# Windowed attention with a routed feed-forward: dilated values loaded on all partitions, their weights written at four offsets

## The chip, the cores and the metric

The kernel runs on one core of a Trainium2 chip. The metric is the device time of one execution in microseconds (us), as the median of several runs. Engines: PE is TensorE (matmuls; PEld is its weight load), DVE is VectorE, ACT is ScalarE, POOL is GpSimd, SP only issues DMAs.

## The reference

Eight batches of eight heads, 576 tokens, 64 dimensions per head, all float32. Heads 0 to 3 attend to the last 32 tokens ("plain"); heads 4 to 7 attend to 32 tokens that are 4 apart ("dilated"). Then, in each batch, the 128 tokens with the highest gate score go through a feed-forward layer, and the result is added to their rows.

```python
rel = pos[:, None] - pos[None, :]
mask_plain = (rel >= 0) & (rel < 32)
mask_dil = (rel >= 0) & (rel < 32 * 4) & (rel % 4 == 0)
scores = np.where(mask, scale * q @ k.T, -1e9)
attn = softmax(scores)
x = (attn @ v).transpose(0, 2, 1, 3).reshape(8, 576, 512)
...
scores = np.einsum('bsd,d->bs', x, w_gate)
for b in range(8):
    top_idx = np.argpartition(-scores[b], 128)[:128]
    ye = np.maximum(x[b, top_idx] @ w1, 0.0) @ w2      # 512 -> 1024 -> 512
    out[b, top_idx] = x[b, top_idx] + sigmoid(scores[b, top_idx])[:, None] * ye
```

## The kernel before

The tokens of the dilated heads are sorted by their residue modulo 4, so that dilated attention too is a band of 32. Every batch has five units u of 128 queries by four heads: u = 0 and 1 are dilated (two residues each), u = 2 and 3 plain, u = 4 holds the last rows of both kinds. A unit works on groups of 32 queries, each of which sees at most 64 keys.

A unit goes through these steps. `scores` (S, lines 300 to 309) writes the mask into PSUM by four matmuls and adds 16 products of q and k (in the trace a float32 matmul is two instructions, so 32). `maximum` and `subtract` (MX, SU) on DVE take the row maximum off. `turn` (TR, line 327) transposes with four matmuls. `exps` (EX, line 334) lets ACT write the exponentials into one of two buffers `pt`, whose other halves were set to zero at the start: keys 0 to 63 of one half of the groups lie on partitions 0 to 63, those of the other half on partitions 64 to 127. `attend` (V, line 347) multiplies with the values on all 128 partitions, two groups at a time; a column of ones beside the values gives the divisor. `divisors` (DN), then the division on DVE (XM) or ACT (XA), `store` (ST) to HBM on SP's queue, and the gate score (GM on POOL and GA on ACT, or GD on DVE alone).

The values of a dilated unit lie in `vd` (tile tag v1), which holds the 128 last keys of each residue twice, in the second copy moved by 32 partitions, so that a group's 64 keys always meet the partitions that its weights lie on. It is filled by four DMAs of 64 partitions (line 287). `vp` (tag v0, line 283) holds the plain values with overlap, `vl` (line 280) the first keys of each residue for u = 4. Loads of q, values and half of k are issued on SP's queue, the other half of k on ACT's. Every tile of q, k (one per kind), vd and vp has one buffer. SP and ACT issue in program order, and eight completion semaphores ("slots") serve all their DMAs in turn: a DMA waits for the one that used its slot last.

When the scores of a batch b are complete, the routing ranks them (RX, RO, SC, SP, SB, RK, RC, RA, MK or MV, PK, IX), `gather` (GT, line 486) fetches the 128 rows from HBM into `xe` by an indirect DMA on POOL's queue, XT transposes them on PE, and XH and XL split them into a high and a low part. Batches are put together as GROUP lines say: F, HH, HL (pairs) or N, RL, HT, HI, HO (single ones) compute the first layer, Y the second, three matmuls for each piece. `result` (YO, line 590) frees `xe`, and `scatter` (SY) writes the rows back. LW, WH or WV, and WL load and split the weights. W n runs n idle matmuls (line 603), which compute nothing.

The order of all this is the table `ORDER`, written out by hand into the file as the output of a planner: the program text follows the table entry by entry, and every engine and queue runs its share in that order.

Of the kernel before, what the change touches and what calls it, by code (L numbers as in the profile page):

```python
# [51 lines left out]
DN 0 4, VL 1 0, GD 0 1, TR 1 0, W 5, GM 0 0, MX 1 1, EX 1 0, SU 1 1, GM 0 2, S 1 3, GA 0 0, XM 0 4, LW 1, GM 0 3,
TR 1 1, GA 0 2, MX 1 3, S 1 4, W 2, RX 0, EX 1 1, SU 1 3, LW 4, GM 0 4, MX 1 4, TR 1 3, K 2 1 1, SU 1 4, S 1 2,
GA 0 3, ST 0 4, TR 1 4, GA 0 4, MX 1 2, V 1 0, SU 1 2, K 2 0 1, WV 1, TR 1 2, EX 1 3, VL 1 1, WV 4, RO 0, WL 1,
DN 1 0, XM 1 0, SC 0, V 1 1, GD 1 0, ST 0 3, WL 4, VL 1 2, SP 0, EX 1 2, DN 1 1, XM 1 1, K 2 1 0, SB 0, GD 1 1, LW 3,
RK 0 0, V 1 2, W 8, LW 2, RK 0 1, EX 1 4, Q 2 1, RK 0 2, RK 0 3, RK 0 4, K 2 0 0, DN 1 2, RC 0, W 2, XM 1 2, WH 3,
ST 1 0, RA 0, V 1 4, GM 1 2, VL 2 0, MV 0, WV 2, PK 0, WL 3, GA 1 2, DN 1 4, S 2 0, IX 0, RX 1, SG 0, XM 1 4, S 2 1,
MX 2 0, ST 1 1, GT 0, SU 2 0, V 1 3, MX 2 1, GM 1 4, TR 2 0, W 3, LW 5, DN 1 3, SU 2 1, EX 2 0, WL 2, XM 1 3, TR 2 1,
Q 2 0, EX 2 1, SH 0, V 2 0, GD 1 3, ST 1 4, GA 1 4, DN 2 0, XT 0, XM 2 0, XH 0, RO 1, GM 2 0, WH 5, V 2 1, XL 0,
LW 7, SC 1, GA 2 0, N 0 0 0, ST 1 3, WL 5, DN 2 1, VL 2 1, S 2 4, SP 1, XA 2 1, MX 2 4, S 2 2, SU 2 4, WV 7, LW 6,  # L60
TR 2 4, MX 2 2, WL 7, S 2 3, SB 1, VL 2 2, SU 2 2, K 3 1 1, N 0 0 1, RK 1 0, EX 2 4, Q 3 1, TR 2 2, RK 1 1, N 0 1 0,
# [675 lines left out]
```

## Time and profile before

| | us |
|---|---|
| time, median of 3 runs (298.64 to 309.14) | 302.31 |
| time of the profiled execution | 297.06 |
| its span, first to last instruction | 295.1 |
| PE busy | 261.2 |
| DVE busy | 166.2 |
| ACT busy | 120.3 |
| POOL busy | 92.5 |

The mean granted PE clock is 0.955 of full speed. The DMA engines moved 57.53 MB. Engines overlap, and a busy share is a mean over stages; waits are read from the stage in which they stand. Matmuls are pipelined, so a busy PE isn't PE at its peak. The releaser named beside an idle time is the one that came last by the profile.

### The profile page before, as it was taken

The numbers are of one execution on the slowest core, as the hardware profiler recorded it, in microseconds if no ns is written. First come the engines' busy times: TensorE is split into PE (matmuls) and PEld (weight loads), VectorE is DVE, ScalarE is ACT, GpSimd is POOL, SyncE is SP. The second block draws the span as 40 slices with busy tenths as digits, with TensorE's granted clock in tenths as the row PEclk, the third lists the DMA queues.
The fourth block names the chain that finished last, engine by engine and source line by source line (L and its number), as shares of the span: only waits on it lengthen the run. The fifth ranks groups of instructions, "written<-read, shape, count | busy, mean of one in ns | idle before, by whom it ended". The sixth has DMA issues, their size and how long they took to land.

```text
span 295.1 us, 8991 instructions
## 1 busy us (share of the span) xinstructions
PE 261.2 (88%) x3738; PEld 216.6 (73%) x3738; DVE 166.2 (56%) x442; ACT 120.3 (41%) x337; POOL 92.5 (31%) x106
## 2 busy tenths in 40 slices
PE   5778785597998999959999979999999999999992
PEld 1465554565876888748879868888878998998881
...
DMA  6998995999999999887995997994422300200000
GB/s 187 228 291 225 328 283 101 278 322 314 334 292 261 269 312 254 242 242 212 239 359 143 278 279 188 318 233 124 174 72 92 109 0 2 71 36 2 36 36 36
DMA packets 24791, 57.53 MB, mean 195 GB/s; under 512 B 3632, under 2 KB 14512, under 8 KB 23728
## 3 DMA queue, kind: packets, MB, share of 16 engines
q1 hardware_dynamic: 21696, 47.96, 56.5%
...
## 4 chain that ended last, share of the span: by engine, by line
PE 34%; DMA 33%; issue 18%; DVE 6%; POOL 3%; ACT 2%; SPq 1%; POOLq 0%; ACTq 0%; DVEq 0%
DMA k<-in_kt_dram 16%; PE a L347 8%; DMA vp<-in_va_dram 8%; PE s L309 6%; PE py L585 6%; DMA out_dram<-x 5%; PE t L327 3%; PE ph L542 3%; DMA xe<-out_dram,ix 3%; DMA q<-in_qt_dram 3%; PE pi L466 2%; PE s L303 2%; ACT x L366 2%; DVE rm L438 1%; POOL out_dram L595 1%
## 5 line engine op out<-in xcount | busy, mean ns | idle before, releaser
L334 ACT ACTIVATE pt<-t 64x512 f32<-64x512 f32 x80 | 47.4, 592 | 69.7 <-PE t L327 51.4
L390 POOL TENSOR_TENSOR gm<-x,wg 128x512 f32<-128x512 f32 x24 | 32.1, 1341 | 78.4 <-ACT x L366 28.5
L309 PE MATMUL s<-k,q 128*32 128x128 f32 (+2 forms) x1216 | 43.5, 276 | 7.3 <-DMA k<-in_kt_dram 5.4
L309 PEld LDWEIGHTS s<-k,q 128*32 128x32 f32 (+1 forms) x1216 | 36.4, 111 | 12.3 <-DMA k<-in_kt_dram 5.2
L314 DVE TENSOR_REDUCE mx<-s 128x8 f32<-128x512 f32 x40 | 27.5, 688 | 22.2 <-PE s L309 22.1
L347 PE MATMUL a<-vp,pt 128*64 128x65 f32 x640 | 29.8, 232 | 9.8 <-DMA vp<-in_va_dram 4.4
L347 PEld LDWEIGHTS a<-vp,pt 128*64 128x64 f32 x640 | 26.4, 144 | 15.9 <-issue 11.5
L366 ACT ACTIVATE x<-a,rin 128x64 f32<-128x64 f32 x104 | 22.8, 333 | 16.8 <-PE a L347 12.1
L542 PE MATMUL ph<-xh,w1h 128*128 128x256 f32 x96 | 28.6, 298 | 0.0
L542 PE MATMUL ph<-xh,w1l 128*128 128x256 f32 x96 | 27.5, 286 | 0.7 <-issue 0.7
L319 DVE TENSOR_TENSOR dt<-s,mx 128x512 f32<-128x512 f32 x40 | 27.1, 682 | 0.9
L542 PE MATMUL ph<-xl,w1h 128*128 128x256 f32 x96 | 27.4, 285 | 0.0
L585 PE MATMUL py<-w2h,hh 128*128 128x512 f32 x64 | 26.9, 420 | 0.0
L327 PE MATMUL t<-id,dt 128*128 128x128 f32 x160 | 25.3, 286 | 0.4 <-DVE rk L450 0.4
L585 PE MATMUL py<-w2l,hh 128*128 128x512 f32 x64 | 25.3, 395 | 0.0
L585 PE MATMUL py<-w2h,hl 128*128 128x512 f32 x64 | 25.3, 395 | 0.0
L347 PE MATMUL a<-vd,pt 128*64 128x65 f32 x512 | 20.2, 231 | 5.3 <-DVE ts L420 3.2
L400 ACT ACTIVATE junk<-gm 128x256 bf16<-128x256 f32 x48 | 20.1, 418 | 11.1 <-POOL gm L390 8.1
L347 PEld LDWEIGHTS a<-vd,pt 128*64 128x64 f32 x512 | 17.7, 143 | 8.6 <-issue 7.1
L460 POOL TENSOR_SCALAR oh<-slots_sb,rk 128x128 f32<-128x128 f32 x20 | 12.1, 618 | 32.5 <-DVE rk L450 32.5
L438 DVE SCALAR_TENSOR_TENSOR rm<-sb,ts,thr 128x576 bf16<-128x576 f32 (+3 forms) x32 | 20.5, 697 | 2.6 <-ACT sb L431 2.6
L327 PEld LDWEIGHTS t<-id,dt 128*128 128x128 f32 x160 | 18.3, 147 | 4.8 <-issue 1.6
...
## 6 DMA issues: line engine op xcount, KB each, us to landing
...
vd<-in_va_dram SPq DMA_DIRECT2D x32, 260.0 KB, 8.3
...
```

Source lines behind the costliest of these rows:

```text
L309: nc.tensor.matmul(st[G * a:G * a + m, e, g, :, lo:hi], qs[b, kind][:, g, q0:q0 + m], ks[kind][:, g::2, k0 + lo:k0 + hi], start=False, sto ...
L314: nc.vector.tensor_reduce(out=mx, in_=X["s", b, u].rearrange("p e g h k -> p (e g h) k"), axis=AX.X, op=ALU.max)
L319: nc.vector.tensor_tensor(out=dt.rearrange("p i (e k) -> p e i k", e=2), in0=st.rearrange("p e g h k -> p e (g h) k"), in1=mx.rearrange("p ...
L327: nc.tensor.transpose(tt[:, i * P:(i + 1) * P], dt[:, i, :], id32)
L334: nc.scalar.activation(pt[r, :, e], tt[r], AF.Exp, scale=SCALE)
L347: nc.tensor.matmul(av[r, a // 2, f], pt[:, i % 2, i // 2, a], values(b, u, a)[:, f], start=True, stop=True)
L366: nc.scalar.activation(xv[:, e, i], av[:, e, i, 0:D], AF.Copy, scale=rin[:, e, i:i + 1])
L390: nc.gpsimd.tensor_tensor(out=gm, in0=X["x", b, u], in1=gate_w(u), op=ALU.mult)
L400: nc.scalar.activation(junk, X["gm", b, u][:, c], AF.Copy, scale=UP, accum_out=acc)
L438: nc.vector.scalar_tensor_tensor(out=out, in0=X["sb", b][:, t * P:S], scalar=ts[:, b, t, 1:2], in1=thr[:, 0:n], op0=ALU.subtract, op1=ALU. ...
L542: nc.tensor.matmul(out, WS1[w][:, i, f * P:(f + 1) * P], X["x" + x, e][:, i, :], start=i == 0 and n == 0, stop=i == 3 and n == 2)
L585: nc.tensor.matmul(X["py", b], X["h" + x, e][:, i, j * P:(j + 1) * P], WS2[w][:, i, :], start=i == 0 and k == 0, stop=i == 7 and k == 2)
```

## The change

The dilated values are loaded once: one DMA fills 128 partitions with 128 keys of four residues, without a second copy. Since a group's 64 keys now lie at partitions 0, 32 or 64 onwards, the weights have to be written there, and `exps` does this for a dilated unit with five activations: two write 64 partitions, three write 32 of them, each 4 heads x 2 residues x 32 queries. The groups of a dilated unit are numbered anew for this, and the first group of each residue, which sees only 32 keys, is masked and computed on these alone. `pt` gets two buffers for dilated units and two for the others; those for dilated units are set to zero as a whole. `vl` gets its buffer from a list that `attend` of unit 4 gives back to. `xe` has three buffers instead of four. The mask and identity are loaded on POOL's queue instead of ACT's.

The table is another one. Its entries of attention and feed-forward are the same ones; the W entries hold 49 idle matmuls instead of 33, two more divisions stand on ACT, three more gate scores on DVE alone, and seven weight parts instead of three are cast on ACT. Of the table only the lines around the gather of batch 6 are shown.

```diff
--- before.py
+++ after.py
@@ -33,8 +33,9 @@
 EPS = 1e-9
 UP = 2.0 ** 24
 TINY = -2.0 ** -126
-BUFS = dict(q1=1, q0=1, v0=1, v1=1, s=2, a=1, m=4, dt=2, x=4, gm=2, xe=4, xh=1, hh=1, raw=2, y=2, oh=1, sb=1, xl=1, hl=1, mx=3, den=3, rin=3, rx=2, g=8, ix=8, junka=1, junkv=1)
+BUFS = dict(q1=1, q0=1, v0=1, v1=1, s=2, a=1, m=4, dt=2, x=4, gm=2, xe=3, xh=1, hh=1, raw=2, y=2, oh=1, sb=1, xl=1, hl=1, mx=3, den=3, rin=3, rx=2, g=8, ix=8, junka=1, junkv=1)
 WARM = 9
+NPT = (2, 2)
 
 
 
@@ -44,64 +45,64 @@
 GROUP 2 3 4
 GROUP 3 5 6
 GROUP 4 7
...
-SH 6, Y 1 6, XL 4, Y 1 7, F 2 0 0, YO 1, F 2 2 0, GT 6, V 7 3, GM 7 2, ST 7 2, F 2 0 1, DN 7 3, XA 7 3, SY 1,
...
+Y 4 4, ST 7 1, SH 6, Y 4 5, GA 7 1, Y 4 6, Y 4 7, RX 7, RO 7, YO 4, Y 3 0, SC 7, GT 6, SP 7, Y 3 1, SB 7, SY 4,
...
 """
 
@@ -140,7 +141,7 @@
     thr = cp.tile([P, S], F32, name="thr")
     ks = [cp.tile([P, 4, S], F32, name=f"k{i}") for i in range(2)]
     vls = [cp.tile([P, 2, VW], F32, name=f"vl{i}") for i in range(2)]
-    pts = [cp.tile([P, 16, 2, G], F32, name=f"pt{i}") for i in range(2)]
+    pts = [cp.tile([P, 16, 2, G], F32, name=f"pt{i}") for i in range(sum(NPT))]
     w1h = cp.tile([P, 4, FF], F32R, name="w1h")
     w1l = cp.tile([P, 4, FF], F32R, name="w1l")
     w2h = cp.tile([P, 8, DM], F32R, name="w2h")
@@ -154,14 +155,16 @@
 
     def constants(i):
         if i == 0:
-            nc.scalar.dma_start(out=mraw, in_=masks)
-            nc.scalar.dma_start(out=id32, in_=ident)
+            nc.gpsimd.dma_start(out=mraw, in_=masks)
+            nc.gpsimd.dma_start(out=id32, in_=ident)
             nc.vector.memset(warm, 0.0)
             nc.vector.memset(mk, NEG)
             for k in (1, 0):
                 nc.vector.memset(ks[k][0:HB, 2:4], 0.0)
                 nc.gpsimd.memset(ks[k][HB:P, 0:2], 0.0)
-            for t in pts:
+            for t in pts[:NPT[0]]:
+                nc.gpsimd.memset(t, 0.0)
+            for t in pts[NPT[0]:]:
                 for e in range(2):
                     nc.gpsimd.memset(t[HB * e:HB * (e + 1), :, 1 - e], 0.0)
 
@@ -170,7 +173,6 @@
                 nc.gpsimd.memset(v[HB + G:P], 0.0)
         elif i == 1:
 
-
             nc.vector.memset(id16, 0.0)
             nc.vector.tensor_copy(id16[0:G], id32[0:G, 0:G])
 
@@ -178,8 +180,8 @@
                 nc.vector.tensor_copy(o[:, :, lo:lo + src.shape[1]], src.unsqueeze(1).to_broadcast([P, o.shape[1], src.shape[1]]))
 
             d, p = mraw[:, 0:GK], mraw[:, GK:2 * GK]
-            put(mk[:, 0, 0:4], G, d[:, 0:G])
-            put(mk[:, 0, 4:8], 0, d)
+            put(mk[:, 0, 0:4], 0, d)
+            put(mk[:, 0, 4:8], 0, d[:, 0:G])
             put(mk[:, 1], 0, d)
             put(mk[:, 2, 0:4], G, p[:, G:GK])
             put(mk[:, 2, 4:8], 0, p)
@@ -244,8 +246,8 @@
 
         x, c = a % 2, a // 2
         if u < 2:
-            r, t = 2 * u + c, 2 * x + e
-            return 1, P * r + G * t, SR * r + SR - G - max(t, 1) * G, 0, GK, G
+            r, t = 2 * u + c, 2 * (1 - e) + x
+            return 1, P * r + G * t, SR * r + SR - G - max(t, 1) * G + (0 if t else G), 0, GK if t else G, G
         if u < 4:
             t = 8 * (u - 2) + 2 * a + e
             return 0, G * t, G * (t - 1), 0 if t else G, GK, G
@@ -271,29 +273,30 @@
 
 
 
+
+    free_vl = list(vls)
+
     def load_v(b, part):
         def flat(v):
             return v.rearrange("k a f -> k (a f)")
 
         if part == 2:
+            X["vl", b] = free_vl.pop(0)
             for h in range(2):
-                nc.sync.dma_start(out=flat(vls[b % 2][HB * h:HB * h + LK]), in_=vb[b, LK * h:LK * (h + 1)])
-        elif part == 1:
-            X["v", b, 0] = v = new("v0", [P, 9, VW], f"vp{b}")
-            nc.sync.dma_start(out=flat(v), in_=va[b, :, 4 * VW:13 * VW])
+                nc.sync.dma_start(out=flat(X["vl", b][HB * h:HB * h + LK]), in_=vb[b, LK * h:LK * (h + 1)])
         else:
-            X["v", b, 1] = v = new("v1", [P, 8, VW], f"vd{b}")
-            for h, x, lo in ((0, 0, HB), (1, 0, HB), (0, 1, G), (1, 1, 0)):
-                nc.sync.dma_start(out=flat(v[HB * h:HB * (h + 1), 4 * x:4 * x + 4]), in_=va[b, lo:lo + HB, 0:4 * VW])
+            lo, n = ((0, 4), (4, 9))[part]
+            X["v", b, part] = v = new(f"v{1 - part}", [P, n, VW], f"v{b}_{part}")
+            nc.sync.dma_start(out=flat(v), in_=va[b, :, lo * VW:(lo + n) * VW])
 
     def values(b, u, a):
 
         x, c = a % 2, a // 2
         if u < 2:
-            return X["v", b, 1][:, 4 * x + 2 * u + c]
+            return X["v", b, 0][:, 2 * u + c]
         if u < 4:
-            return X["v", b, 0][:, 4 * (u - 2) + a]
-        return X["v", b, 0][:, 8] if x == c else vls[b % 2][:, x]
+            return X["v", b, 1][:, 4 * (u - 2) + a]
+        return X["v", b, 1][:, 8] if x == c else X["vl", b][:, x]
 
 
     def scores(b, u):
@@ -327,17 +330,24 @@
             nc.tensor.transpose(tt[:, i * P:(i + 1) * P], dt[:, i, :], id32)
 
     def exps(b, u):
-        tt = X.pop(("t", b, u)).rearrange("k (i q) -> k i q", q=G)
-        X["pt", b, u] = pt = free.pop(0)
-        for e in range(2):
-            r = slice(HB * e, HB * (e + 1))
-            nc.scalar.activation(pt[r, :, e], tt[r], AF.Exp, scale=SCALE)
-
-    free = list(pts)
+        tt = X.pop(("t", b, u))
+        X["pt", b, u] = pt = free[u < 2].pop(0)
+        if u < 2:
+            tt, pt = (v.rearrange(f, c=2, x=2, **k) for v, f, k in ((tt, "k (i c x q) -> k x (i c) q", dict(q=G)), (pt, "k (i c x) e q -> k x e (i c) q", {})))
+            for o, n, lo, x, y, e in ((0, HB, 0, 1, 1, 1), (HB, HB, HB, 1, 0, 1), (G, G, 0, 0, 1, 0), (HB, G, G, 0, 1, 0), (HB + G, G, HB, 0, 0, 0)):
+                nc.scalar.activation(pt[o:o + n, y, e], tt[lo:lo + n, x], AF.Exp, scale=SCALE)
+        else:
+            for e in range(2):
+                r = slice(HB * e, HB * (e + 1))
+                nc.scalar.activation(pt[r, :, e], tt[r].rearrange("k (i q) -> k i q", q=G), AF.Exp, scale=SCALE)
+
+    free = {True: pts[:NPT[0]], False: pts[NPT[0]:]}
 
 
     def attend(b, u):
-        free.append(X["pt", b, u])
+        free[u < 2].append(X["pt", b, u])
+        if u == 4:
+            free_vl.append(X["vl", b])
         pt = X.pop(("pt", b, u)).rearrange("k (g h a) e q -> k g h a (e q)", g=2, h=2)
         X["a", b, u] = av = ps.tile([P, 2, 512], F32, tag="a", bufs=BUFS["a"], name=f"a_{b}_{u}")
         for i in range(4):
```

Three places in the order of instructions. First SP, from the first value load of batch 1 on: before.

```order
L287 DMA vd_555<-in_va_dram 64x1040 x4
L494 DMA raw_612<-in_w_dram 128x1024
L496 DMA raw_653<-in_w_dram 128x2x512
L377 DMA out_dram<-x_4_610 64x256
L381 DMA out_dram<-x_4_610 16x256 x4
L283 DMA vp_736<-in_va_dram 128x2340
L375 DMA out_dram<-x_3_400 128x2x256
L280 DMA vl_83<-in_vb_dram 48x520 x2
L267 DMA k_81<-in_kt_dram 64x1152
```

The same place now, `vl_82` being already the last rows of batch 2.

```order
L290 DMA v_0_428<-in_va_dram 128x1040
L383 DMA out_dram<-x_1_426 128x2x256
L264 DMA q_0_494<-in_qt_dram 128x1152
L383 DMA out_dram<-x_0_263 128x2x256
L504 DMA raw_549<-in_w_dram 128x1024
L286 DMA vl_83<-in_vb_dram 48x520 x2
L286 DMA vl_82<-in_vb_dram 48x520 x2
L385 DMA out_dram<-x_3_598 128x2x256
L290 DMA v_1_647<-in_va_dram 128x2340
L269 DMA k_81<-in_kt_dram 64x1152
L387 DMA out_dram<-x_4_522 64x256
L391 DMA out_dram<-x_4_522 16x256 x4
```

Four dilated loads (`vd_555`) became one (`v_0_428`), and the plain values of batch 1 (`vp_736`, now `v_1_647`), which stood behind the five stores of batch 0's unit 4 (`x_4`), stand ahead of them.

Second ACT, from the first exponentials of batch 0 on; `t_0`, `t_3`, `t_2`, `t_1` are the turned scores of units 0, 3, 2 and 1: before.

```order
L334 ACTIVATE pt_84<-t_0_198 64x16x32 x2
L334 ACTIVATE pt_85<-t_3_233 64x16x32 x2
L366 ACTIVATE x_0_287<-a_0_259,rin_0_284 128x64 x8
L334 ACTIVATE pt_84<-t_2_276 64x16x32 x2
L267 DMA k_80<-in_kt_dram 64x1152
L267 DMA k_81<-in_kt_dram 64x1152
L334 ACTIVATE pt_85<-t_1_390 64x16x32 x2
```

And now, up to units 4 and 2.

```order
L338 ACTIVATE pt_84<-t_0_183 64x8x32 x2
L338 ACTIVATE pt_84<-t_0_183 32x8x32 x3
L376 ACTIVATE x_0_263<-a_0_205,rin_0_260 128x64 x8
L269 DMA k_81<-in_kt_dram 64x1152
L338 ACTIVATE pt_85<-t_1_326 64x8x32 x2
L338 ACTIVATE pt_85<-t_1_326 32x8x32 x3
L269 DMA k_80<-in_kt_dram 64x1152
L342 ACTIVATE pt_86<-t_4_333 64x16x32 x2
L342 ACTIVATE pt_87<-t_2_381 64x16x32 x2
```

A dilated unit has five activations where it had two, and a unit's buffer is no longer that of the unit two before it.

Third the start, on POOL: before.

```order
L163 MEMSET k_81 64x1152
L163 MEMSET k_80 64x1152
L166 MEMSET pt_84 64x16x32 x2
L166 MEMSET pt_85 64x16x32 x2
L169 MEMSET vl_82 32x520
L170 MEMSET vl_82 32x520
```

Now, up to the same tile.

```order
L158 DMA mraw<-in_masks_dram 128x128
L159 DMA id_66<-in_ident_dram 128x128
L164 MEMSET k_81 64x1152
L164 MEMSET k_80 64x1152
L166 MEMSET pt_84 128x1024
L166 MEMSET pt_85 128x1024
L169 MEMSET pt_86 64x16x32 x2
L169 MEMSET pt_87 64x16x32 x2
L172 MEMSET vl_82 32x520
L173 MEMSET vl_82 32x520
```

Two loads and larger memsets stand ahead of the memset of `vl_82`. On SP the load of that tile, which has to follow its memset, moved from behind `vp_231` to the fourth place.

```order
L269 DMA k_81<-in_kt_dram 64x2x288
L264 DMA q_1_129<-in_qt_dram 128x2x256
L269 DMA k_80<-in_kt_dram 64x1152
L286 DMA vl_82<-in_vb_dram 48x520 x2
L290 DMA v_0_144<-in_va_dram 128x1040
L269 DMA k_81<-in_kt_dram 64x2x288
L264 DMA q_1_129<-in_qt_dram 128x2x320
L264 DMA q_0_179<-in_qt_dram 128x1152
```

## Rows read from the trace of the kernel before

**Rows 1.** The page's picture of the span in 40 equal slices, two of its rows: PE, and the mean busy share of the 16 DMA engines, each digit a tenth.
```profile
PE   5778785597998999959999979999999999999992
...
DMA  6998995999999999887995997994422300200000
```

**Rows 2.** The chain that ended last, shares of the span by engine, from the page.
```profile
PE 34%; DMA 33%; issue 18%; DVE 6%; POOL 3%; ACT 2%; SPq 1%; POOLq 0%; ACTq 0%; DVEq 0%
```

**Rows 3.** Stages cut where the first score matmul of batches 1 to 7 starts, the last to the end of the span: start and end, length, then busy us (and instructions) of PE, its weight load, DVE, ACT and POOL, granted PE clock, DMA share, GB/s.
```profile
0.00:30.00 30.00, 22.69 (x346) 14.35 (x346) 16.05 (x33) 10.05 (x21) 14.61 (x39) 0.94 0.91 232
30.00:64.40 34.40, 25.15 (x407) 18.71 (x403) 22.85 (x55) 12.66 (x33) 13.67 (x9) 0.85 0.92 260
64.40:92.70 28.30, 24.47 (x414) 19.25 (x414) 22.34 (x55) 14.21 (x37) 17.83 (x13) 1.00 1.01 310
92.70:114.20 21.50, 21.50 (x386) 18.36 (x384) 15.33 (x48) 12.55 (x38) 4.48 (x5) 1.00 0.94 279
114.20:142.60 28.40, 24.16 (x438) 20.50 (x438) 18.39 (x54) 12.09 (x32) 6.78 (x5) 0.88 0.87 227
142.60:168.80 26.20, 25.69 (x461) 23.08 (x458) 19.91 (x56) 14.57 (x44) 8.82 (x10) 1.00 0.89 256
168.80:190.40 21.60, 19.09 (x356) 16.33 (x355) 12.30 (x33) 10.90 (x34) 3.54 (x3) 0.92 0.92 262
190.40:295.10 104.70, 98.43 (x953) 86.03 (x949) 39.05 (x113) 33.26 (x101) 22.81 (x25) 0.99 0.25 76
```

**Rows 4.** The timeline of PE, four matmul groups that PE waited for: start, us, line, operands, count, and in brackets the idle time before and its releaser.
```profile
50.75 2.00 PE L347 MATMUL a<-vd,pt 128*64 128x65 f32 x32 [3.23 <-DVE ts L420]
...
57.09 2.00 PE L347 MATMUL a<-vp,pt 128*64 128x65 f32 x32 [3.08 <-DVE rm L438]
...
133.44 0.34 PE L347 MATMUL a<-vp,pt 128*64 128x65 f32 x1 [3.82 <-DMA vp<-in_va_dram]
...
171.68 1.08 PE L309 MATMUL s<-k,q 128*32 128x128 f32 x32 [2.51 <-DMA k<-in_kt_dram]
```

**Rows 5.** The timeline of SP's DMA queue around batch 1: start, us (with waits between the parts of a group), line, what is moved, count.
```profile
41.07 9.30 SPq L381 DMA_DIRECT2D out_dram<-x  x4
50.47 0.37 SPq L283 DMA_DIRECT2D vp<-in_va_dram  x1
```

**Rows 6.** What SP's DMA queue waited for: us in total, times, longest.
```profile
SPq L381 <- DMA k<-in_kt_dram: 22.3, 6, 7.3
...
SPq L283 <- PE a L347: 6.4, 4, 2.9
```

**Rows 7.** One stage, columns as in group 3.
```profile
44.30:59.00 14.70, 8.04 (x115) 7.19 (x109) 8.81 (x29) 3.07 (x6) 4.69 (x2) 0.69 0.75 189
```

**Rows 8.** DMA queues (packets, MB, share of 16 engines' span) and issues (count, KB each, median us to landing), one row of each, from the page.
```profile
q1 hardware_dynamic: 21696, 47.96, 56.5%
...
vd<-in_va_dram SPq DMA_DIRECT2D x32, 260.0 KB, 8.3
```

**Rows 9.** Groups by line on ACT: the exponentials and the gate sums; busy us, mean ns, idle before and releasers.
```profile
L334 ACT ACTIVATE pt<-t 64x512 f32<-64x512 f32 x80 | 47.4, 592 | 69.7 <-PE t L327 51.4 <-PE a L347 16.2 <-PE s L309 1.3
...
L400 ACT ACTIVATE junk<-gm 128x256 bf16<-128x256 f32 x48 | 20.1, 418 | 11.1 <-POOL gm L390 8.1 <-PE s L309 0.8 <-PE pw L603 0.6
```

**Rows 10.** What ACT waited for before its exponentials: us in total, times, longest.
```profile
ACT pt L334 <- PE t L327: 51.4, 22, 11.6
...
ACT pt L334 <- PE a L347: 16.2, 7, 5.8
```

**Rows 11.** Two pieces of the chain that ended last, in order of time: start, us, what.
```profile
215.19 0.44 PE pa L426 x4
...
218.80 2.75 PE py L585 x12
```

**Rows 12.** Groups by line: gather issue on POOL, result on DVE, idle matmuls on PE; busy us, mean ns.
```profile
L603 PE MATMUL pw<-warm 128*128 128x512 bf16 x42 | 13.7, 464 | 1.2 <-DVE warm L159 1.2
...
L486 POOL DMA_INDIRECT xe<-out_dram,ix x8 | 8.5, 1068 | 25.3 <-DVE y L590 11.8 <-DMA out_dram<-x 5.0 <-DVE g L479 4.7
...
L590 DVE SCALAR_TENSOR_TENSOR y<-py,g,xe 128x512 f32<-128x512 f32 x8 | 6.0, 750 | 27.1 <-PE py L585 27.1
```

**Rows 13.** DMA issues on POOL's and ACT's queues, the last number the median us to landing.
```profile
xe<-out_dram,ix POOLq DMA_INDIRECT x8, 5.5
...
out_dram<-y,ix POOLq DMA_INDIRECT x8, 3.0
...
id<-in_ident_dram ACTq DMA_DIRECT2D x1, 64.0 KB, 3.6
```

**Rows 14.** The timeline of all engines at the start, columns as in groups 4 and 5.
```profile
0.79 2.05 POOL L163 MEMSET k<- 64x1152 f32 x2 [0.29 <-POOLq L726]
...
4.96 5.56 SPq L287 DMA_DIRECT2D vd<-in_va_dram  x4
...
5.75 0.53 POOL L170 MEMSET vl<- 32x520 f32 x1
...
9.58 1.94 PE L309 MATMUL s<-k,q 128*32 128x128 f32 x32 [1.52 <-DMA k<-in_kt_dram]
...
10.56 0.60 SPq L267 DMA_DIRECT2D k<-in_kt_dram  x1
...
18.50 1.12 PE L347 MATMUL a<-vd,pt 128*64 128x65 f32 x30 [1.48 <-DMA vd<-in_va_dram]
```

More of the change, by code (lines that the diff above doesn't have):

```diff
@@ L52 @@
[L52 to L61, printed above, removed]
@@ new lines @@
+V 2 4, RA 1, HT 0 0, DN 2 4, ST 1 3, MK 1, XM 2 4, N 0 1 3, HI 0 0, LW 5, V 2 2, RL 0 1, HO 0 0, HT 0 1, DN 2 2,
+WH 6, VL 3 1, XM 2 2, Y 0 0, GM 2 4, PK 1, GD 2 2, HI 0 1, Y 0 1, SG 1, SH 1, WL 6, S 3 0, GA 2 4, IX 1, HO 0 1,
+ST 2 4, RO 2, MX 3 0, SU 3 0, S 3 1, WH 5, GT 1, SC 2, VL 4 2, SP 2, MX 3 1, WL 5, TR 3 0, SU 3 1, SB 2, EX 3 0,
+TR 3 1, W 3, RK 2 0, Q 3 0, RK 2 1, ST 2 3, Y 0 2, EX 3 1, ST 2 2, RK 2 2, V 3 0, RK 2 3, RK 2 4, XT 1, DN 3 0,
+XM 3 0, RC 2, XH 1, Y 0 3, RA 2, GM 3 0, MV 2, V 3 1, ST 3 0, XL 1, GA 3 0, PK 2, VL 4 0, DN 3 1, XM 3 1, S 3 4,
@@ new lines @@
+SC 3, XA 4 0, S 4 3, ST 3 3, F 1 0 2, MX 4 3, K 5 0 0, Q 5 0, SU 4 3, F 1 0 3, K 5 0 1, GD 4 0, V 4 1, EX 4 2, Y 0 7,
+DN 4 1, XM 4 1, ST 4 0, SP 3, HH 1 0, YO 0, V 4 2, VL 5 0, SB 3, GD 4 1, SY 0, S 5 1, RK 3 0, S 5 0, ST 4 1, DN 4 2,
+RK 3 1, TR 4 3, RK 3 2, TR 4 4, EX 4 3, F 1 2 0, RK 3 3, RK 3 4, F 1 2 1, EX 4 4, XM 4 2, RC 3, MX 5 0, V 4 3,
+ST 4 2, MX 5 1, F 1 2 2, RA 3, DN 4 3, MV 3, XA 4 3, F 1 2 3, GD 4 2, PK 3, F 1 3 0, IX 3, SU 5 1, GT 3, F 1 3 1,
+SG 3, SU 5 0, HH 1 2, V 4 4, GM 4 3, ST 4 3, SH 3, RX 4, HL 1 2, S 5 4, VL 5 1, DN 4 4, GA 4 3, HL 1 0, S 5 2,
@@ new lines @@
+XA 4 4, MX 5 4, TR 5 1, MX 5 2, K 6 1 0, TR 5 0, F 1 3 2, SU 5 2, Q 6 1, F 1 3 3, SU 5 4, EX 5 0, GD 4 4, TR 5 2,
+S 5 3, ST 4 4, EX 5 2, RO 4, MX 5 3, SU 5 3, V 5 0, EX 5 1, K 6 0 0, SC 4, SP 4, DN 5 0, Q 6 0, XM 5 0, HH 1 3,
+TR 5 3, GM 5 0, V 5 1, SB 4, HL 1 3, ST 5 0, EX 5 3, RK 4 0, VL 5 2, TR 5 4, Y 2 0, DN 5 1, VL 6 0, K 6 1 1, XM 5 1,
+Y 1 0, K 6 0 1, GA 5 0, RK 4 1, Y 1 1, V 5 2, RK 4 2, ST 5 1, RK 4 3, F 1 1 0, RK 4 4, EX 5 4, DN 5 2, XM 5 2,
+F 1 1 1, GD 5 1, RC 4, V 5 3, ST 5 2, RA 4, RX 5, MK 4, GD 5 2, F 1 1 2, DN 5 3, S 6 1, XA 5 3, S 6 4, MX 6 1,
@@ new lines @@
+F 1 1 3, SU 6 1, MX 6 4, PK 4, HH 1 1, GM 5 3, SU 6 4, S 6 3, ST 5 3, SG 4, SH 4, IX 4, HL 1 1, S 6 0, GA 5 3,
+MX 6 3, TR 6 4, K 7 1 1, K 7 1 0, MX 6 0, TR 6 1, EX 6 4, V 5 4, Q 7 1, SU 6 0, SU 6 3, EX 6 1, TR 6 0, DN 5 4,
+VL 6 1, S 6 2, XA 5 4, TR 6 3, MX 6 2, Y 1 2, SU 6 2, Y 1 3, Y 1 4, K 7 0 0, K 7 0 1, GD 5 4, V 6 1, EX 6 0, S 7 0,
+DN 6 1, XM 6 1, ST 5 4, EX 6 3, S 7 1, MX 7 0, GM 6 1, SU 7 0, TR 6 2, MX 7 1, GA 6 1, TR 7 0, ST 6 1, V 6 0, SU 7 1,
+EX 7 0, Q 7 0, Y 1 5, DN 6 0, XM 6 0, VL 7 0, Y 1 6, GM 6 0, VL 7 2, TR 7 1, V 6 3, EX 7 1, ST 6 0, Y 1 7, DN 6 3,
```

84 lines of the change are left out of this document (37 added, 47 removed).

## The prediction, made before the changed kernel was run

> **What bounds the kernel now.** I read the 40 slices first [rows 1]: the DMA line stands at 9 almost without a break for the first two thirds, and then falls to 0 to 3 while TensorE (PE) stands at 9. The chain that ended last says the same in shares: DMA 33% of the span, PE 34% [rows 2]. Next I cut the span where each batch's first score matmul starts [rows 3]. Up to 190.4 us, where batch 7 starts, the DMA share is 0.87 to 1.01. Weighting the GB/s of these seven rows by their lengths gives 49.5 MB in 190.4 us, 0.260 MB per us; from row to row the rate stays within 0.227 to 0.310, whatever the engines do. From 190.4 us to the end PE is busy for 98.4 of 104.7 us. So there are two regimes: transfers set the pace of the batches, and after them a queue of feed-forward matmuls sets the end. A microsecond won before 190 us moves the start of that queue, and with it the end; the queue itself does not get shorter.
>
> How much can be won in the first regime? PE busy in the seven rows is 162.8 of 190.4 us, so 27.6 us idle, of which 7.3 in the first 30 us. The granted clock is 0.85, 0.88 and 0.92 in three rows, that is half speed (1.2 of 2.4 GHz) for 0.30, 0.24 and 0.16 of them, 10.3, 6.8 and 3.5 us, which cost half of that, 10.3 us. Idle after 30 us (20.3) and slow clock together make 30.6 us; nothing that only removes waits after the start can bring more.
>
> The waits behind this [rows 4]: an attend of batch 1 stands 3.23 us and the next 3.08 us, put down to DVE instructions whose results attend does not read, so another releaser stands behind them; the second starts 6.6 us after the load of the plain values was issued [rows 5], so it is that load. Later one attend waits 3.82 us for plain values, and scores 2.51 us for k. The load of batch 1 came late because SP works in order: four small stores held SP from 41.07 to 50.37 us [rows 5], each waiting until an earlier transfer's slot came free [rows 6]. In the stage around this the granted clock is 0.69 [rows 7].
>
> **The loads.** Four loads of 260 KB per batch become one of half their sum, and SP issues three DMAs fewer per batch. Dropped over eight batches: 16 x 260 KB = 4.26 MB. At 0.260 MB/us this is 16.4 us of transfer time. As a second way, the SP queue took 56.5% of 295.1 us, 166.7 us, for 47.96 MB [rows 8], so 4.26 MB take 14.8 us. Batch 0's half lies in the start, where something else sets the pace (below), so I count 7/8 of 16.4: **-14.3 us**. Bounds: 0, if the loads sat beside other work, and -30.6, all waits.
>
> **The order on SP.** In batch 1 the plain values now stand ahead of the stores that held SP, as the rows of the order show. In the stage from 44.3 to 59.0 us the DMA share is only 0.75 [rows 7]; a quarter of 14.7 us is transfer time given away by the hold. I count it as regained, **-3.7 us**; bounds 0 and -11.4 (both waits, 6.3 us, and half of the 10.3 us at half speed). That other stalls of the kind move elsewhere is left to the rivals.
>
> **The exponentials.** A dilated unit had two activations of 64x512 at 592 ns, 1.18 us; it gets five of 256 elements per partition. Before has none of these from PSUM; the nearest row with 256 is the gate sum, 418 ns, and 592 is the bound above [rows 9]. At 418 ns five take 2.09 us, 0.91 more per unit, 14.5 us more over 16 units. ACT is busy for 87.0 us in the first seven stages [rows 3], 46%, and sat 51.4 us before exponentials waiting for the turn, 16.2 us waiting for attend to free a buffer [rows 10]; that idle time covers the work as a whole. It isn't covered where attend follows its turn closely: then attend waits 0.91 us longer. From the order I count three such units (dilated unit 0 of batches 0, 2 and 3), **+2.7 us**; bounds 0 and +14.5. The weight buffers go from two to four, so the 16.2 us largely go; since those waits lie in the hole of batch 1 and beside loads, I count nothing for them again.
>
> **The gather buffers.** Three instead of four: the gather of batch 6 (GT 6) now has to follow the result of batch 4 (YO 4), three being the rotation of batches. In the new order seven Y pieces and one row transpose stand on PE between YO 4 and the turn XT 6. A Y piece is 3 matmuls, 2.75/4 = 0.69 us, the row transpose at least 0.44 us [rows 11]: 5.3 us of cover. What it must cover is 0.75 us for the result, 1.07 us to issue the gather and 5.5 us to land [rows 12, 13], 7.3 us. The rest is a PE wait of 2.0 us, and what is late next is XT 6 and all Y and F behind it: **+2.0 us**, bounds 0 and +4.0 (the same again at batch 4, whose gather now follows the result of batch 1).
>
> **The start.** The mask and the identity go from ACT's queue to POOL's, ahead of its memsets. Nearest row for a POOL issue: 1.07 us each, landing 3.0 to 5.5 us against 3.6 from ACT [rows 12, 13]. POOL's first work starts at 0.79 us [rows 14], so the identity lands between 5.9 us (0.8 + 2.1 + 3.0) and 8.4 us; scores waited until 9.58 us for k anyway [rows 14], so at worst the mask copies behind it show, 1 us. Next, SP's fourth place is now batch 0's last-rows load, which waits for POOL's memset of its tile. That was done at 5.75 + 0.53 = 6.3 us; ahead of it now lie 2.1 us of issue and two whole memsets of 1,024 elements (0.9 us each by the two of 1,152 elements, 2.05 us together [rows 14]), so SP stands until about 10.3 us, with the dilated values, the rest of k and q, and plain q behind it. But SP stood before too, in the four value loads, from 4.96 to 10.52 us, and issued the rest of k at 10.56 us [rows 14]. First attend waited until 18.50 us for its values; one load issued at 12 us lands by then if it takes 6.5 us; the loads of half its size took 8.3 us, four at a time [rows 8]. I count 0, bounds -2 and +3.
>
> A rule speaks against this move: the Trainium skill (DMA: Bandwidth & Descriptors, Specifications) gives the first byte about 1 us on the GpSimd path and 0.6 us from SP or ACT, and its table under Issuing engine by pattern sends simple loads to Sync. No run so far shows a plain load from POOL; by the page the loss would be an estimated 0.4 us, and the sum 0.4 us higher.
>
> **Idle matmuls.** The order holds 16 more of them. At 464 ns [rows 12] they could cost 7.4 us; most stand in the first batches ahead of waits for values. **+1 us.**
>
> **Sum.** 297.06 - 14.3 - 3.7 + 2.7 + 2.0 + 1.0 = 284.8 us against the profiled execution's own time. That execution lies 1.8% under the median of 302.31; on the median's scale the forecast is 284.8 x 302.31 / 297.06 = 289.8 us, which I round to 289.5.
>
> **Rivals**, each on the median's scale.
> (a) The forecast, its own range 283 to 296: chance 0.58.
> (b) The transfers stop binding for good and the hole of batch 1 goes whole: -14.3 - 11.4 + 5.7 = -20.0, 277.1, **282 us**. For it: four weight buffers let ACT run ahead, and PE ran at 100% from 92.7 to 114.2 us, when it had feed-forward work. Against it: the share of DMA stays high in every stage, and later batches also stall. 0.15.
> (c) The change saves bytes, but time does not follow: the loads wait for buffers (k, q and values have one each) and for SP, not for the bytes. SP waited 6.4 us for attend before loading plain values [rows 6]. Then 297.06 - 3.7 + 5.7 = 299.1, **304 us**. Against it: a rate so even over stages with different work is that of a full resource. 0.17.
> (d) Slower: ACT's in-order queue becomes the path of the batches. Every dilated unit's five exponentials then delay its attend, 14.5 us, and loads of k issued from the same queue go out later, so the saved transfer time isn't used: 297.06 + 14.5 + 3.0 = 314.6, **320 us**. It decides where ACT has no idle left before exponentials in the middle stages; there ACT is busy for 11 to 15 us in rows of 21 to 34 us, so it would need nearly twice its work. 0.10.
>
> A measurement of this kernel can tell about 2% from no change (its three runs span 298.64 to 309.14). Faster by over 2% means under 296.3: all of (b) and nearly all of (a), 0.71; within 2%: (c) and the edge of (a), 0.19; slower: (d), 0.10. For 8 in 10 I leave out (d), the upper edge of (c) and the far end of (b): 277 to 303 us.
>
> **What would show it.** Right: batch 7's first scores start near 175 us instead of 190.4; SP's queue moves 4.26 MB less at a DMA share still near 0.9; one value load of 520 KB lands in under 8 us; batch 1's plain values are issued well before 50 us; the dilated exponentials take 0.40 to 0.45 us; at XT 6 PE waits for the gather. Wrong: first scores of batches 5 to 7 where they were, with SP waiting for attend or for slots; ACT's waits for the turn near zero; a first attend after 21 us; or a lowered clock in new stretches.

## The result and the profile after

| | before | changed |
|---|---|---|
| median of 4 runs, us | 300.60 (298.64 to 309.14) | 283.46 (282.07 to 284.52) |
| profiled execution, us | 297.06 | 284.52 |
| its span, us | 295.1 | 282.8 |
| ACT busy in it, us | 120.3 | 135.7 |
| MB moved | 57.53 | 53.28 |

The ratio is 0.946 with a 95% interval of 0.938 to 0.955. Ratios and intervals, here and below, are taken over the faster runs of each kernel alone, so they can differ a little from the quotient of the medians beside them, which are of all runs. The forecast was 0.958 of the median known then, 289.5 us in a range of 277 to 303; on that scale (302.31 us) the measured ratio is 286.1 us.

The stages of the changed kernel, cut like those of [rows 3] where the first score matmul of batches 1 to 7 starts; columns as there:

```profile
0.00:27.90 27.90, 22.62 (x315) 13.81 (x315) 15.54 (x28) 9.37 (x24) 17.82 (x44) 0.94 0.80 224
27.90:57.30 29.40, 23.73 (x444) 17.29 (x440) 17.84 (x47) 18.72 (x54) 11.28 (x8) 1.00 0.88 248
57.30:92.50 35.20, 32.65 (x480) 26.31 (x478) 24.21 (x65) 22.13 (x60) 19.23 (x15) 0.90 0.91 296
92.50:115.90 23.40, 22.28 (x389) 17.70 (x388) 19.12 (x48) 13.09 (x35) 9.74 (x7) 1.00 0.77 226
115.90:134.30 18.40, 17.56 (x357) 15.32 (x356) 13.34 (x37) 8.59 (x24) 0.31 (x1) 1.00 0.97 273
134.30:164.60 30.30, 30.10 (x524) 27.11 (x522) 24.54 (x79) 17.27 (x51) 5.83 (x7) 1.00 0.78 236
164.60:178.50 13.90, 13.90 (x280) 11.82 (x280) 8.84 (x20) 9.97 (x35) 2.90 (x4) 1.00 0.63 202
178.50:282.80 104.30, 97.06 (x995) 84.07 (x992) 41.49 (x126) 36.57 (x114) 26.37 (x31) 1.00 0.27 87
```

Batch 7 starts at 178.5 us instead of 190.4, 11.9 us earlier, and the last stage has its old length (104.3 against 104.7): the end moved with the start of the queue. PE is busy for 162.8 us until then in both kernels. So the whole shift is PE's idle time, 15.7 us in the seven stages instead of 27.6. Beside the first stage, at 0.94 in both kernels, one stretch remains with a lowered granted clock, in the third stage (0.90); of the three in [rows 3] those around batches 4 and 6 are gone.

After 92.5 us PE now hardly waits: until batch 7 it is busy for 83.8 of 86.0 us, at a DMA share of 0.79. The long waits that are left stand in batches 0 to 2. Four of them, in the timeline of PE, columns as in [rows 4]:

```profile
15.15 1.15 PE L357 MATMUL a<-v,pt 128*64 128x65 f32 x32 [0.89 <-DMA v<-in_va_dram]
...
40.37 0.81 PE L312 MATMUL s<-k,q 128*32 128x128 f32 x20 [1.87 <-DMA q<-in_qt_dram]
...
48.85 0.27 PE L357 MATMUL a<-v,pt 128*64 128x65 f32 x1 [1.17 <-DMA v<-in_va_dram]
...
59.61 1.23 PE L312 MATMUL s<-k,q 128*32 128x128 f32 x32 [1.94 <-DMA q<-in_qt_dram]
```

All four name loads; one more, 1.24 us at 29.59 us, names nothing. The longest of all, 2.52 us at the start for the copies of the mask, is shown with the start below. The rows that answer to [rows 8], the SP queue's transfers, and to [rows 9, 10], the exponentials by their forms and their waits:

```profile
q1 hardware_dynamic: 20288, 43.70, 50.5%
```

```profile
L342 ACT ACTIVATE pt<-t 64x512 f32<-64x512 f32 x48 | 28.4, 593 | 20.0 <-PE t L330 11.0 <-PE a L357 6.0 <-PE s L312 2.4
...
L338 ACT ACTIVATE pt<-t 32x256 f32<-32x256 f32 x48 | 18.0, 374 | 0.6
...
L338 ACT ACTIVATE pt<-t 64x256 f32<-64x256 f32 x32 | 12.1, 379 | 25.2 <-PE t L330 23.6 <-PE s L312 1.3
```

The SP queue moved 4.26 MB less, and its transfers took 50.5% of 282.8 us, 142.8 us, instead of 166.7. The exponentials of a dilated unit take 3 x 374 + 2 x 379 = 1,880 ns instead of 1,184. ACT's wait for attend to free a buffer fell from 16.2 to 6.0 us.

### The profile page after: what moved, and what is told of

Its sections match the earlier page's. It is cut to its first block, busy times and chain, and to the rows that moved or that the text cites. A ratio compares the mean times of both kernels' runs of the same rounds, so it can differ in the third digit from the quotient of the medians.

```text
span 282.8 us, 9049 instructions
## 1 busy us (share of the span) xinstructions
PE 259.9 (92%) x3754; PEld 213.4 (75%) x3754; DVE 164.9 (58%) x447; ACT 135.7 (48%) x393; POOL 93.5 (33%) x112
## 2 busy tenths in 40 slices
DMA packets 23160, 53.28 MB, mean 188 GB/s; under 512 B 3120, under 2 KB 13872, under 8 KB 22096
## 3 DMA queue, kind: packets, MB, share of 16 engines
q1 hardware_dynamic: 20288, 43.70, 50.5%
## 4 chain that ended last, share of the span: by engine, by line
PE 52%; DMA 17%; issue 15%; POOL 6%; DVE 4%; SPq 3%; ACT 1%; POOLq 1%; DVEq 0%
PE a L357 10%; PE s L312 10%; PE ph L552 9%; DMA q<-in_qt_dram 8%; PE py L595 8%; DMA k<-in_kt_dram 5%; PE t L330 5%; DMA v<-in_va_dram 3%; PE s L306 3%; PE pi L476 3%; PE pr L424 2%; DMA out_dram<-x 2%; POOL out_dram L605 1%; DVE junk L407 1%; PE pa L436 1%
## 5 line engine op out<-in xcount | busy, mean ns | idle before, releaser
L357 PEld LDWEIGHTS a<-v,pt 128*64 128x64 f32 x1152 | 41.1, 138 | 14.1 <-issue 6.9
L357 PE MATMUL a<-v,pt 128*64 128x65 f32 x1152 | 46.5, 225 | 4.4 <-DMA v<-in_va_dram 2.1
L400 POOL TENSOR_TENSOR gm<-x,wg 128x512 f32<-128x512 f32 x21 | 27.4, 1307 | 59.3 <-DVE x L378 29.4
L338 ACT ACTIVATE pt<-t 32x256 f32<-32x256 f32 (+1 forms) x80 | 30.1, 376 | 25.8 <-PE t L330 23.6
L342 ACT ACTIVATE pt<-t 64x512 f32<-64x512 f32 x48 | 28.4, 593 | 20.0 <-PE t L330 11.0
L376 ACT ACTIVATE x<-a,rin 128x64 f32<-128x64 f32 x120 | 26.3, 331 | 14.2 <-PE a L357 9.2
L470 POOL TENSOR_SCALAR oh<-slots_sb,rk 128x128 f32<-128x128 f32 x25 | 15.0, 613 | 34.9 <-DVE rk L460 34.4
L366 DVE TENSOR_SCALAR den<-a 128x8 f32<-128x8 f32 x40 | 6.5, 163 | 32.6 <-PE a L357 29.5
L605 POOL DMA_INDIRECT out_dram<-y,ix x8 | 8.0, 1006 | 50.8 <-DVE y L600 49.9
L407 DVE CUSTOM_DVE_ANT_0 junk<-x,wg 128x256 bf16<-128x256 f32 x38 | 21.4, 563 | 2.7 <-ACT x L376 0.9
```

The costliest lines, as they stand in the source:

```text
L338: nc.scalar.activation(pt[o:o + n, y, e], tt[lo:lo + n, x], AF.Exp, scale=SCALE)
L342: nc.scalar.activation(pt[r, :, e], tt[r].rearrange("k (i q) -> k i q", q=G), AF.Exp, scale=SCALE)
L357: nc.tensor.matmul(av[r, a // 2, f], pt[:, i % 2, i // 2, a], values(b, u, a)[:, f], start=True, stop=True)
L376: nc.scalar.activation(xv[:, e, i], av[:, e, i, 0:D], AF.Copy, scale=rin[:, e, i:i + 1])
L400: nc.gpsimd.tensor_tensor(out=gm, in0=X["x", b, u], in1=gate_w(u), op=ALU.mult)
L407: nc.vector.tensor_tensor_reduce(out=junk, in0=X["x", b, u][:, c], in1=gate_w(u)[:, c], scale=UP, scalar=0.0, op0=ALU.mult, op1=ALU.add, a ...
```

## The experiments

Times are medians; each group of runs (e0 to e3, e4 to e7, e8 to e11) has its own runs of the kernel before on the same chip, with medians of 297.74, 297.76 and 300.28 us, and the ratio to those is what is compared; e4 to e7 are set against e0 across groups. "Packed mask" runs differ from the changed kernel in storage alone:

```diff
-    mk = cp.tile([P, 5, 8, GK], BF16, name="mk")
+    mk = cp.tile([P, 5, 2, GK], BF16, name="mk")
-    warm = cp.tile([P, 512], BF16, name="warm")
+    warm = cp.tile([P, P], BF16, name="warm")
```

**e0, the reference of the others.** 

> The changed kernel with the mask tile and the tile of the idle matmuls stored without their repeats, read by broadcast, which frees 4.9 KB per partition that the runs beside it need. Every theory expects the changed kernel's time, 282 to 285 us (0.94 to 0.95 of before); its difference from that is the correction for the others.

Measured: 283.92 us, 0.953 (0.946 to 0.960). It stands for the changed kernel in the next runs.

**e1, the new table with the old loads**: the body of before with four buffers in one list.

```diff
-            X["v", b, part] = v = new(f"v{1 - part}", [P, n, VW], f"v{b}_{part}")
-            nc.sync.dma_start(out=flat(v), in_=va[b, :, lo * VW:(lo + n) * VW])
+            for h, x, lo in ((0, 0, HB), (1, 0, HB), (0, 1, G), (1, 1, 0)):
+                nc.sync.dma_start(out=flat(v[HB * h:HB * (h + 1), 4 * x:4 * x + 4]), in_=va[b, lo:lo + HB, 0:4 * VW])
```

> The new table, three gather buffers, constants on POOL and four weight buffers, but the old loads (four of 260 KB per batch) and the old two exponentials. Theory A, the bytes: the dropped 4.26 MB make most of the gain, so this loses about 14 us against the changed kernel less 3 us of saved exponentials, 293 to 298 us. Theory B, the order: the new table and the four buffers make the gain and the bytes sit beside other work, 281 to 286 us.

Measured: 293.83 us, 0.985 (0.979 to 0.992).

**e2, the old table with the new loads.** Its edit is the table of before in the changed kernel, and `xe=4`. 

> The old table with the new loads, the five exponentials, constants on POOL and four gather buffers as the old table needs them. Theory A, the bytes: the old table too gains about 14 us less 3 to 5 us for the exponentials, 288 to 292 us. Theory B, the order: 298 to 304 us, no gain or a small loss by the exponentials.

Measured: 287.80 us, 0.964 (0.954 to 0.973). Together with before at 297.74 in the same group, the four kernels give a square. The loads with their exponentials are worth 9.9 us under the old table (297.74 to 287.80) and 9.9 us under the new one (293.83 to 283.92); the table, with the buffers that it needs, is worth 3.9 us either way. The two add up, and theory A holds for the greater part. Each of these differences is uncertain by some 3 us, since the intervals reach 0.7 to 1.0% to either side; that they agree to a tenth is luck, and the intervals of e2 and e0 overlap.

**e3, the old bytes.**

```diff
+            if part == 0:
+                nc.sync.dma_start(out=spare, in_=va[b, :, 0:4 * VW])
```

> The changed kernel with one more load of 520 KB per batch behind each load of dilated values, into a tile that nothing reads: the old number of bytes, two DMAs for them where before had four. Theory A, the bytes: +10 to +15 us, 294 to 299 us. Theory B, the order: under +3 us, 283 to 287 us.

Measured: 289.43 us, 0.970 (0.962 to 0.977): 5.5 us, less than theory A and more than theory B. Bytes alone don't make up the 9.9 us, which made the form of the loads the next question.

**e5, the new bytes in halves.**

```diff
-            nc.sync.dma_start(out=flat(v), in_=va[b, :, lo * VW:(lo + n) * VW])
+            for r in (slice(0, HB), slice(HB, P)) if part == 0 else (slice(0, P),):
+                nc.sync.dma_start(out=flat(v)[r], in_=va[b, r, lo * VW:(lo + n) * VW])
```

> The changed kernel (packed mask) with each load of dilated values cut into two of 64 partitions: the same bytes, one DMA more per batch. If the form of the old loads (64 partitions, more slots) cost time beside their bytes: 286 to 288 us. If only bytes count: 283 to 285 us.

Measured: 285.12 us, 0.953 (0.942 to 0.963), no difference that can be told.

**e6, the old bytes in the old form**: e5 and, for dilated values, the same two halves once more into the spare tile.

```diff
+                for r in (slice(0, HB), slice(HB, P)):
+                    nc.sync.dma_start(out=spare[r], in_=va[b, r, 0:4 * VW])
```

> The changed kernel (packed mask) with four loads of 64 partitions per batch, two into the values and two into a tile that nothing reads: the old bytes in the old form, with everything else new. If the form counts beside the bytes: 293 to 299 us, about the 293.8 us of the new table with the old loads and two exponentials plus what the exponentials cost. If only bytes count: 288 to 291 us, as with one more load of 128 partitions (289.4).

Measured: 294.37 us, 0.989 (0.982 to 0.995), 10.5 us over e0, and 4.9 us over e3, which moves the same bytes in whole loads. So the form counts at the end, where it comes together with the bytes. The SP queue's row, first of e0, then of e5, then of e6:

```profile
q1 hardware_dynamic: 20288, 43.70, 49.6%
```

```profile
q1 hardware_dynamic: 20416, 43.70, 51.3%
```

```profile
q1 hardware_dynamic: 21696, 47.96, 55.7%
```

With spans of 283.2, 283.6 and 293.2 us these are 140.5, 145.5 and 163.3 us. The same 43.70 MB take 5.0 us more when the values come in halves (e5), which the kernel absorbs; 4.26 MB more in halves take another 17.8 us, which it doesn't.

One place where added transfers show is PE's wait for the gathered rows of batch 2, which the profile of the changed kernel itself does not have; first in e0, then in e6:

```profile
114.51 0.66 PE L531 MATMUL px<-id,xe 128*128 128x128 f32 x4 [2.39 <-DMA xe<-out_dram,ix]
```

```profile
124.65 0.90 PE L536 MATMUL px<-id,xe 128*128 128x128 f32 x4 [4.22 <-DMA xe<-out_dram,ix]
```

Batch 7 starts at 189.4 us in e6 and at 179.0 us in e0.

**e7, fewer bytes still.**

```diff
+            if part == 0 and b:
+                X["v", b, 0] = X["v", 0, 0]
+                return
```

> The changed kernel (packed mask) that loads the dilated values of batch 0 alone and uses them for all batches, so that another 3.7 MB and seven DMAs are left out and the dilated heads of batches 1 to 7 get the wrong values. If transfers still set the pace of the changed kernel: -5 us or more, 275 to 279 us. If PE's work does, as its unbroken busy time after 62 us says: 281 to 284 us.

Measured: 279.03 us, 4.9 us under e0, with no interval. Its four runs, 275.94, 276.84, 281.21 and 282.43 us, lie two in the range of the first theory and two in that of the second, but all of them under the lowest of e0, 282.79. So transfers still set part of the pace of the changed kernel; how much these runs don't tell, since they lie 1.5 to 8.0 us under e0's median. The four waits above say where, in batches 0 to 2: in the profiled run (275.94 us) batch 3 starts at 85.9 us instead of 90.0 in e0, and batch 7 at 171.3 instead of 179.0.

**e4, the cost of the exponentials.**

```diff
-            for o, n, lo, x, y, e in ((0, HB, 0, 1, 1, 1), (HB, HB, HB, 1, 0, 1), (G, G, 0, 0, 1, 0), (HB, G, G, 0, 1, 0), (HB + G, G, HB, 0, 0, 0)):
-                nc.scalar.activation(pt[o:o + n, y, e], tt[lo:lo + n, x], AF.Exp, scale=SCALE)
+            for e in range(2):
+                r = slice(HB * e, HB * (e + 1))
+                nc.scalar.activation(pt[r, :, e], tt[r].rearrange("k (i q) -> k i q", q=G), AF.Exp, scale=SCALE)
```

> The changed kernel (packed mask) in which a dilated unit's weights are written by two exponentials of 64x512 as before, at the old partitions; the weights of dilated units then meet the wrong values, so this run is for its time alone. My term: the five exponentials cost 2.7 us on the path, so 280 to 283 us against 283.9. Rival, ACT's queue is the path of the batches: all 11 us of extra ACT work come back, 272 to 276 us. Rival, they are hidden: 283 to 285 us.

Measured: 281.35 us, 0.944 (0.937 to 0.952), 2.6 us under e0. The difference is where my term put it; the two intervals overlap, so no cost at all is not excluded, but the 8 to 12 us of the rival are. ACT's busy time fell from 135.7 us in the changed kernel to 124.4, 11.3 us.

**e8, the order term alone**, in the kernel before:

```diff
-GA 0 3, ST 0 4, TR 1 4, GA 0 4, MX 1 2, V 1 0, SU 1 2, K 2 0 1, WV 1, TR 1 2, EX 1 3, VL 1 1,
+GA 0 3, VL 1 1, ST 0 4, TR 1 4, GA 0 4, MX 1 2, V 1 0, SU 1 2, K 2 0 1, WV 1, TR 1 2, EX 1 3,
```

> The kernel before with one entry of its table moved: the load of batch 1's plain values stands ahead of the five stores of batch 0's unit 4. My order term: SP's stall no longer delays that load and 3.7 us come back, 293 to 295 us (0.98 to 0.99 of before). Rival: the stores and what stands behind them only move their own wait later, 296 to 299 us. Bound, the whole hole goes: 286 us.

Measured: 297.08 us against 300.28, 0.998 (0.991 to 1.006): no difference that can be told, and the forecast 3.7 us (0.988) lie outside the interval. SP's queue in it, columns as in [rows 5], and the wait of PE that follows:

```profile
39.45 0.34 SPq L283 DMA_DIRECT2D vp<-in_va_dram  x1
40.60 0.51 SPq L377 DMA_DIRECT2D out_dram<-x  x1
41.82 10.32 SPq L381 DMA_DIRECT2D out_dram<-x  x4
...
55.31 0.42 SPq L262 DMA_DIRECT2D q<-in_qt_dram  x1
```

```profile
63.05 1.93 PE L309 MATMUL s<-k,q 128*32 128x128 f32 x32 [3.17 <-DMA q<-in_qt_dram]
```

The edit did what it says: the plain values went out at 39.45 us instead of 50.47, and attend no longer waits for them. But the stores then held SP for 10.32 us instead of 9.30, and what stands behind them, q of batch 2, went out no sooner than in the kernel before:

```profile
55.12 0.45 SPq L262 DMA_DIRECT2D q<-in_qt_dram  x1
```

```profile
65.07 1.08 PE L309 MATMUL s<-k,q 128*32 128x128 f32 x32 [0.24 <-DMA q<-in_qt_dram]
```

There its lateness was hidden behind the wait for the plain values; now PE waits 3.17 us for it. So the stall changed its victim. The mask matmuls that open batch 2 and batch 7 in e8:

```profile
59.48 0.40 PE L303 MATMUL s<-mk,id 128*32 128x512 bf16 x4
...
190.76 0.40 PE L303 MATMUL s<-mk,id 128*32 128x512 bf16 x4
```

In the kernel before they start at 64.43 and 190.42 us. Batch 2 starts 5.0 us earlier, batch 4 1.8 us (112.42 instead of 114.22) and batch 7 not at all: what was won in one batch was lost again in the next ones.

**e9, e10 and e11, the start and one queue entry**, in the changed kernel. The first hunk, the two constants back on ACT's queue, is in e9 and e11; the second, q of batch 2 ahead of the stores, in e10 and e11; the third, the order of the first loads, in e11 alone:

```diff
-            nc.gpsimd.dma_start(out=mraw, in_=masks)
-            nc.gpsimd.dma_start(out=id32, in_=ident)
+            nc.scalar.dma_start(out=mraw, in_=masks)
+            nc.scalar.dma_start(out=id32, in_=ident)
...
-GM 0 2, TR 1 4, DN 1 0, GA 0 3, XM 1 0, S 1 3, W 1, K 2 1 0, WL 0, SU 1 2, GA 0 2, ST 0 4,
+GM 0 2, TR 1 4, DN 1 0, GA 0 3, XM 1 0, S 1 3, W 1, K 2 1 0, WL 0, SU 1 2, GA 0 2, Q 2 1, ST 0 4,
-W 11, GM 1 4, Q 2 1, K 2 0 1,
+W 11, GM 1 4, K 2 0 1,
...
-C 1, VL 0 2, VL 0 0,
+C 1, VL 0 0,
-MX 0 0, Q 0 0, SU 0 0,
+MX 0 0, Q 0 0, VL 0 2, SU 0 0,
```

> The changed kernel with the mask and the identity loaded on ACT's queue again. My start term: no difference, 0.945 to 0.95 of before, 282 to 284 us. Rival, POOL's issue holds SP's value load back: -2 us, 281 us. Rival, ACT's issue holds the first k back and counts: +2 us.

> The changed kernel with one entry moved: the load of batch 2's dilated q stands ahead of the five stores of batch 0's unit 4, since in the changed kernel PE waits for it at 59.6 us and the clock is at half speed behind that wait. If the wait and the slow clock go: -3 to -5 us, 277 to 281 us. If the transfers as such set the pace up to there: 282 to 284 us.

> Both edits together, and the load of batch 0's last rows behind q on SP, so that the first value load no longer waits for POOL's memsets. If start and queue order add: 0.92 to 0.935 of before, 275 to 279 us. If transfers set the pace of the first batches whatever their order: 281 to 284 us.

Measured against 300.28 us: e9 280.48, 0.936 (0.928 to 0.945); e10 281.54, 0.940 (0.930 to 0.949); e11 280.41, 0.936 (0.927 to 0.945). The interval of each overlaps that of the changed kernel (0.938 to 0.955), so none of the three is shown to be faster than it; against e0 (0.946 to 0.960, on another chip) those of e9 and e11 don't overlap. They don't add up either: e11 holds both edits and stands where e9 stands. e11 is 6.4% faster than the kernel before; that it gains a per cent on the changed kernel would need a measurement of the two side by side, and stays open.

For e10 the profiled run (283.55 us, the highest of its six) shows what became of the wait:

```profile
51.02 0.37 PE L357 MATMUL a<-v,pt 128*64 128x65 f32 x1 [3.70 <-DMA out_dram<-x]
...
61.11 1.05 PE L312 MATMUL s<-k,q 128*32 128x128 f32 x32
```

The scores of batch 2 no longer wait for q, but the attend that waited 1.17 us for its values in the changed kernel (48.85 us above) now waits 3.70 us, with q issued 3.1 us behind those values (the releaser named is a store, which attend doesn't read), and the scores start at 61.11 us instead of 59.61. It is the pattern of e8 again, seen in one run. In e11 batch 2 starts 5.3 us earlier than in the changed kernel (51.93 instead of 57.27), batch 7 1.9 us (176.58 instead of 178.49).

## Why the prediction was right, step by step

**The sum: right in direction, a little small, and partly by luck.** Forecast were -12.3 us in all. The square gives -13.8 (297.74 to 283.92 us), and the measured ratio 16.2 us on the forecast's scale where 12.8 were forecast; the forecast 0.958 lies just above the interval of 0.938 to 0.955. That the profiled runs agree to 0.3 us (284.8 forecast, 284.52 measured) comes of misses that cancel: batch 7 started 3.4 us later than the terms make it, and the wait of 2.0 us behind it didn't come.

**Two regimes: right, the first only up to 92.5 us.** The first scores of batch 7 were forecast near 175 us and came at 178.5; the queue behind kept its length. In all fourteen profiles it lasts 102.5 to 104.7 us, wherever batch 7 starts between 171.3 and 194.1. But from 92.5 us to batch 7 PE is busy for 83.8 of 86.0 us, so transfers hardly set the pace there any more, and over the whole first regime the DMA share fell from 0.92 to 0.83, where the forecast had it near 0.9. In that rival (b), transfers that stop binding, was half right; its 282 us are 4.1 from the measured 286.1, the forecast's 289.5 are 3.4. That they stop for good is contradicted by the waits in batches 0 to 2 and by e7. Rival (c), bytes that save no time, is excluded by e2 and e1; rival (d), ACT as the path, by e4.

**The loads, -14.3: near in size, with half of the mechanism.** 9.9 us in both halves of the square, and 2.6 more for the exponentials paid within it, make 12.5 us. It is right partly by luck: I priced the bytes alone, at the mean rate, 14.8 to 16.4 us of transfer time, and counted all of it as won. The bytes as such are worth 5.5 us at the end (e3), the form of the loads another 4.9 (e6 against e3), which I had at nothing; each is uncertain by some 3 us. On the queue 23.9 us went (166.7 to 142.8), and only half of that showed at the end. The two errors cancel.

**The order on SP, -3.7: the step that failed.** I counted the quarter of a stage in which DMA stood idle as regained by moving one load. e8 moves just that and gains nothing that can be told (0.998), because q of batch 2, which stays behind the stores, was late as well, and the later batches gave back what was left of the gain. The table as a whole is worth 3.9 us all the same (e1, e2); that this is near the 3.7 is luck. Which of its moves brings it was not separated. The four weight buffers don't seem to: e2 and e0 both have them and still differ by 3.9 us, though with an uncertainty of some 3 us.

**The exponentials, +2.7: right as far as can be told**, 2.6 by e4, with nothing at all not excluded. The duration was 375 ns instead of 418, so the added ACT work was 11.1 us rather than 14.5; idle time on ACT covers most of it.

**The gather buffers, +2.0: no wait came.** The timeline of POOL and of PE in the changed kernel, gather and turn of batch 6:

```profile
232.78 1.03 POOL L496 DMA_INDIRECT xe<-out_dram,ix  x1 [3.94 <-DVE y L600]
```

```profile
238.28 0.60 PE L531 MATMUL px<-id,xe 128*128 128x128 f32 x4
```

POOL did wait for the result of batch 4, as the step says, 3.94 us. But the gathers land in a median of 3.8 us in the changed kernel, not 5.5, so this one was there at about 237.6 us (an estimate from the median), and the turn follows other work without a gap; nor does it wait in any other profile of the new table. The term was mis-sized by the landing time, 1.7 us too long, and by the cover: the result of batch 4 starts at 231.75 us, 6.5 us ahead of the turn, where I counted 5.3.

**The start, 0: right within what can be measured.** The timeline of all engines at the start:

```profile
1.34 0.73 POOL L158 DMA_DIRECT2D mraw<-in_masks_dram  x1 [0.84 <-POOLq L736]
2.07 0.61 POOL L159 DMA_DIRECT2D id<-in_ident_dram  x1
...
7.80 0.53 PE L306 MATMUL s<-mk,id 128*32 128x512 bf16 x4 [2.52 <-DVE mk L180]
...
8.98 0.57 POOL L172 MEMSET vl<- 32x520 f32 x1
...
9.57 0.91 SPq L286 DMA_DIRECT2D vl<-in_vb_dram  x2
```

SP stood until 9.57 us, forecast 10.3, and the first attend had its values at 15.15 us instead of 18.50; batch 1 started at 27.95 us instead of 29.88. The issues took 0.73 and 0.61 us, not 1.07. The first-byte rule that I weighed (the Trainium skill, DMA: Bandwidth & Descriptors, Specifications) would make this move a loss of 0.4 us, an estimate; e9, which takes the move back, is 1.0% lower with overlapping intervals, so it neither shows nor excludes that loss. In its profile SP stands only until 7.53 us, and the first attend starts at 14.39, 0.8 us earlier.

**Idle matmuls, +1:** not tested apart. Their busy time rose from 13.7 to 18.3 us, and PE's busy time before batch 7 is the same in both kernels, 162.8 us.
